# Passing on finished small operations at the end of each two-bank block of an attention kernel

## The chip, the core and the metric

The kernel runs on one NeuronCore of a Trainium2 chip. The core has a matrix engine (PE, with its weight loads shown as PEld), a vector engine (DVE), a scalar engine (ACT), a general engine (POOL) and a queue engine (SP) that issues most of the memory transfers (DMAs). The metric is the device time of one launch in microseconds (us); lower is better.

## The reference, cut to what matters

`x` has 2048 rows of 512 numbers. A modulation vector gives six rows (`sa, ca, ga, sb, cb, gb`).

```
h  = layernorm(x) * (1 + ca) + sa
x  = x + ga * (attention(h, wqkv) @ wo)      # 32 heads of 16 numbers, all 2048 rows against all 2048
h  = layernorm(x) * (1 + cb) + sb
x  = x + gb * mixer_and_mlp(h, w1, w2, w3, w4)
```

Attention is `softmax(q k^T / 4) v` for each head. What matters here is the softmax: for every query row, the kernel finds the largest score over all 2048 keys first, and subtracts it before the exponential. It does so by computing all scores twice: once to find the maxima, and once more, with the negated maximum added inside the matrix product, to feed the exponential.

## The kernel before, in words

**Units and steps.** The 2048 query rows are four chunks of 512, and the 32 heads are 16 pairs. One pair on one chunk is a *unit*: 64 units. A unit has 16 steps, one for each 128 keys; `s` counts the 1024 steps of all units. A step has two *row pairs*, one for each head: `row_pair` (L1039) puts on PE one score matmul of step `s` (`score_part`, L1037, tile `sc`) and beside it one maximum matmul of step `s + 24` (`max_part`, L1022, tile `mb`). So the maxima of a unit are computed 24 steps ahead of its scores: the last of them falls into the 8th of the 16 steps of the unit before.

**What follows on the other engines.** ACT takes the exponential of each score tile (L1033, into `pt`). A second operation on `pt` (`p_low`) runs on POOL (L1086) or, when the planner finds POOL further behind than ACT, on ACT (L158). DVE reduces each maximum tile (L1016 with two banks, 128x1024; L1014 with one). The probabilities go back to PE against `vst` (L1108, L1111), and once a unit ACT copies the accumulated result (`ac`, L1128).

**The shift rows.** When the maxima of unit `u` are complete, `max_fin` (L1053) starts a chain of small operations: DVE L1066, ACT L1068 and L1069, POOL L1070, whose result is the tile `nm`; then `shift_rows` (L1058), which issues eight small DMAs on SP (`qtl<-nm`, 1 KB each) that write the negated maxima as rows into the query tile `qtl` of unit `u`; then a mark that says so. The first score matmul of unit `u` reads those rows, so it waits for these DMAs.

**Other transfers on SP.** `load_unit(u)` (L963) issues four DMAs: two `qtl<-Qs` (96 KB each) and two `kst<-Ks` (384 KB each). There are three buffers of each, so they wait until the scores of unit `u - 3` are done. They are placed by `before` (L1606) at step `16u - 32`, which is the first step of unit `u - 2`. `load_v(u)` (L972, `vst<-Vs`, 768 KB, two buffers) is placed at step `16u - 6`. SP executes its instructions strictly in the order in which they are placed, and each waits for what it needs.

**The planner.** All this order is written out while the program is built, by a small scheduler (`Sched`). It keeps an estimated clock for each engine (`T["P"]` for PE and so on) and lists of waiting work: `chains` of small operations, `gens` (generators with background matmuls), `pend` (things to be told at a time). `misc` (L173) emits the next operations of chains that fit an engine. An entry of a chain that has no engine, such as `shift_rows` or a mark, is emitted only by `marks` (L161), and only if the planner's PE clock has passed the estimated end of the operation before it plus 200 ns:

```
    def marks(self):
        now = self.T["P"]
        ...
        for ch in list(self.chains):
            while ch[1] and ch[1][0][0] is None and ch[0] <= now:
                ch[1].pop(0)[2]()
```

Before the change `marks` has one caller, `one` (L215), which otherwise runs the next piece of a generator. `one` is called by `gap` (L205, when the planner sees a pause of 500 ns or more ahead), by `fill` (L236) and by `step` (L297), which `drain` repeats until a mark is there.

**The main loop** (from L1627 on) goes over blocks of row pairs. In the first 256 steps a block has three row pairs and one-bank maxima. From step 256 to step 994, units 16 to 61, a block has two row pairs (one step) and the maxima use two banks at once (`layout([2, 2, 1, 1, 1])`, L1693); the last 30 steps have three again. `two` is true in the middle stage. At the first row pair of a unit a block does this, in this order:

```
                if x == blk[0]:
                    before(x // 2)
                if x >= 0 and x % 32 == 0:
                    drain(("shift", x // 32))
```

and at its end, after its matmuls:

```
        elif sch.gens:
            ...
                sch.fill(due)
```

So `fill` runs only while there are generators. In the middle stage there are few: `o_fin` (L1132), eight small matmuls for a finished unit, and `tail_loads` (L1299), which is added at step 884.

Of the kernel before, what the change touches and what calls it, by code (L numbers as in the profile page):

```python
# [332 lines left out]
def kernel(ctx, tc, A_x, A_wqkv, A_wo, B_w1, B_w2, B_w3, B_w4, c, w_mod, out):  # L333
# [89 lines left out]
    sch = Sched()  # L423
# [479 lines left out]
    def drain(flag):  # L903
        while flag not in done:
            sch.step()
# [72 lines left out]
    def layout(sizes):  # L978

        while sch.owner:  # L980
            sch.step()
        bkx.close()
        psd["d"] = bkx.enter_context(tc.tile_pool(name="bk", bufs=1, space=PSUM))
        sm.sizes, sm.t = sizes, [sch.T["P"]] * len(sizes)
# [54 lines left out]
    def row_pair(s, j):  # L1039

        parts = []
        if 0 <= s < NS:
            parts.append(score_part(s, j))
        if s + LEAD < NS:
            parts.append(max_part(s + LEAD, 1 - j))

        def mms():
            for _, mm, _ in parts:
                mm()
        e = sch.put("P", CROW, max(x[0] for x in parts), mms)  # L1050
        return [partial(x[2], e) for x in parts]
# [21 lines left out]
    def p_low(s):  # L1073

        p = pt[s].rearrange("p j n -> p (j n)")
        o, i = p.bitcast(F16)[:, 0::2], p.bitcast(U16)[:, 0::2]
        ready = e_exp.pop(s) + XX
        g, a = [max(sch.T[e], ready) for e in "GA"]
        if g > a + LACT:

            for h in range(NLOW):
                n = 2 * CH // NLOW
                c = slice(h * n, (h + 1) * n)
                e_low[s] = XP["A"] + sch.crit("A", CLOW, ready, partial(act.activation, o[:, c], i[:, c], AF.Copy, scale=0.5))
        else:
            e_low[s] = XP["G"] + sch.crit("G", 1345, ready, lambda: pool.tensor_scalar(  # L1086
                o, i, 0.5, 1.0, op0=OP.mult, op1=OP.mult))

    def pv_ready(s, lo):

        return max(e_low[s], e_low[s + 1]) if lo else max(e_hi.pop(s), v_free[0] if s % NKT == 0 else 0.0)

    def pv_part(s, lo):


        u, kt = divmod(s, NKT)
        if kt == 0 and not lo:
            pv[u] = ap_.tile([P, CH], F32, name="pv", tag="v", bufs=1)
        v, acc = vst[u], pv[u]

        def mms():
            for j in range(2):
                for i in range(2):
                    r = 64 * j + 32 * i
                    if lo:
                        c = 128 + 32 * j + (0 if i else 8)
                        n = min(32, 192 - c)
                        te.matmul(acc[r:r + n, :], v[:, kt + i, c:c + n].bitcast(F16), pt[s + i].bitcast(F16)[:, j, 0::2],  # L1108
                                  start=False, stop=kt == NKT - 2, skip_group_check=True)
                    else:  # L1110
                        te.matmul(acc[r:r + 32, :], v[:, kt, r:r + 32], pt[s].bitcast(F16)[:, j, 1::2],  # L1111
                                  start=kt == 0, stop=False, skip_group_check=True)
        e = sch.put("P", CCOL, 0.0, mms)
        if lo:
            for i in range(2):
                pt.pop(s + i)
                e_low.pop(s + i)
            if kt == NKT - 2:
                acs.append((u, e + COUT))

    def ac_copy():
        u, e = acs.pop()
        while u and ("ot", u - 1) not in done:
            sch.step()
        ac = at.tile([P, CH], F32, name="ac", tag="ac", bufs=1)
        vst.pop(u)
        acc = pv.pop(u)
        e = sch.crit("A", cA(), e + PX, lambda: act.activation(ac, acc, AF.Copy))  # L1128
        v_free[0] = e + XP["A"]
        sch.add(o_fin(u, ac, e + XP["A"]), 0)  # L1130
# [168 lines left out]
    def tail_loads():  # L1299
        rings["0"] = Ring(FRONT, [], "r")  # L1300
        for _ in range(BR):
            rings["0"].add([("wr", BR)])
            yield sch.wait(T0W)
        for t in range(TPC):
            x1t[t] = fa.tile([P, D], F32, name="x1", tag="x1", bufs=X1F)
            act.dma_start(x1t[t], x_d[t * P:(t + 1) * P])
# [299 lines left out]
    def before(s):  # L1606

        nu, r = divmod(s + 32, 16)
        if r == 0 and 0 < nu < NU:
            ci, pr = units[nu]  # L1610
            drain(("kq", pr // 4))
            if ci:
                drain(("q", pr // 8))
            load_unit(nu)
        nu, r = divmod(s + 6, 16)
        if r == 0 and 0 <= nu < NU:
            drain(("v", units[nu][1] // 8))
            load_v(nu)
        if s == -12:
            unit_tiles(at, 2, dve, pool)  # L1620
# [7 lines left out]
    for k, blk in enumerate(blocks + [[]] * (LAG + CPER)):  # L1628
        if blk and blk[0] <= LENDS <= blk[-1]:
            sch.most = MOST  # L1630
        for x in blk:
            if x % 2 == 0:
# [4 lines that stand above are left out]
        if acs:  # L1637
            ac_copy()
        row = [divmod(x, 2) for x in blk if x < 2 * NS]
        s0 = row[0][0] if row else 0  # L1640
        col = []
        if k >= LAG and (k % CPER == 0 or not blk):

            x = (blocks[min(k - (LAG2 if 2 in sm.sizes else LAG), len(blocks) - 1)] or [-1])[-1]
            while pvs and 2 * (pvs[0][0] + pvs[0][1]) < x and not (col and pvs[0][0] % NKT == 0 and not pvs[0][1]):
                col.append(pvs.pop(0))
        t, start = CIN, 0.0
        two = 2 in sm.sizes
        need = 4 if two else sum((s >= 0) + (s + LEAD < NS) for s, _ in row)
        sch.flush(need)  # L1650
        banks = sorted(sm.t)
        n = 0
        for s, i in row[:2 if two else GRP]:
            n += (s >= 0) + (s + LEAD < NS)

            start = max(start, (max(sm.t[sm.take()], sm.t[sm.take(2)]) if two else banks[n - 1 + 2 * (s < 0)]) - t)
            t += CROW
        t += CROW * len(row[2:]) if two else 0.0
        t += CMID
        for s, i in col:  # L1660
            start = max(start, pv_ready(s, i) - t)
            t += CCOL
        sch.gap(start)
        sch.flush(need)
        sch.T["P"] = max(sch.T["P"], start) + CIN
        low = sorted(e_exp)
        for s, i in row:
            for fn in row_pair(s, i):
                fn()
        for x in blk[1:]:  # L1670
            if x % 2 == 0:
                before(x // 2)
        for s in low:
            p_low(s)
        sch.T["P"] += CMID
        for s, i in col:
            pv_part(s, i)
        sch.T["P"] += COUT
        for e in "ADG":
            sch.misc(e, max(sch.T["P"], sch.T[e]) + TOLE[e])  # L1680
        if s0 < 0:
            sch.fill(LEADB / 2 * len(blk))
        elif sch.gens:
            late = s0 >= NS - T0S
            due += RATE3 if late else RATE if s0 < NS // NC else RATE2
            if due >= (BURST3 if late else BURST if s0 < NS // NC else BURST2):
                sch.fill(due)
                due = 0.0
        if 2 * (NS // NC) - 1 in blk:
            for key in (("v", 1), ("kq", 3), ("q", 0), ("q", 1), "pieces"):  # L1690
                drain(key)
            qpx.close()
            layout([2, 2, 1, 1, 1])  # L1693
            sch.gapmin = GAPMIN2
            ot = o0x.enter_context(tc.tile_pool(name="ot", bufs=1, side="right"))
            for ci in range(1, NC):
                oh[ci] = ot
                osb[ci] = ot.tile([P, TPC, D], F32, name=f"osb{ci}", tag=f"osb{ci}", bufs=1)
            fa = o0x.enter_context(tc.tile_pool(name="fa", bufs=1, side="right"))
            big = {"A4": fa.tile([P, 4 * KT * 2 * P], F32R, name="A")}  # L1700
            big["A"] = big["A4"]
        if blk and blk[0] <= 2 * (NS - T0L) <= blk[-1]:
            sch.add(tail_loads())
        if blk and blk[-1] == 2 * (NS - T0S) - 1:
            layout([1] * NSM)
        if blk and blk[0] <= 2 * (NS - T0S) <= blk[-1]:
            sch.add(tail(0))
# [55 lines left out]
```

## Time and profile before

| what | us |
|---|---|
| median of 3 runs | 2565.2 (2559.43 to 2567.64) |
| the profiled execution's own time | 2569.12 |
| its span, first to last instruction | 2567.3 |
| PE busy | 2042.7 (80%) |
| DVE busy | 1637.4 (64%) |
| ACT busy | 1580.5 (62%) |
| POOL busy | 1538.0 (60%) |

The span is what the profile shows; the launch's own time is 1.8 us longer. The middle stage, from the first score matmul of unit 16 at 548.83 us to that of unit 62 at 2017.16 us, is 1468.33 us of the span. A row of a window query gives the stretch, its length, the busy time of each engine with its number of instructions in brackets, then the granted clock of PE as a share of full speed, the DMA engines' share and GB/s. In a timeline row the first number is the start, the second the length; a bracket at its end tells how long the engine had been idle before and what ended that.

### The profile page before, as it was taken

To read this page: it belongs to the slowest core of one execution; us is meant where nothing else is said; L and a number is where in the kernel's file an instruction comes from. 1 tells how busy PE (TensorE), PEld (TensorE's weight loads), DVE (VectorE), ACT (ScalarE), POOL (GpSimd) and SP (SyncE) were. 2 spreads that over 40 slices of the span, in tenths; PEclk is the share of its full clock that TensorE was granted. 3 is DMA by queue.
4 is the path that set the end of the run, shared out by engine and by line. 5 is a ranking of instruction groups with operands and counts; after the bars stand their busy time and mean duration, and the time that the engine had idled before them with its cause. 6 is when DMAs were issued, how large, how long until landed. Compare 5 with 4: busy or idle time off the path is not lost.

```text
span 2567.3 us, 40747 instructions
## 1 busy us (share of the span) xinstructions
PE 2042.7 (80%) x14456; PEld 1154.8 (45%) x14456; DVE 1637.4 (64%) x2241; ACT 1580.5 (62%) x3118; POOL 1538.0 (60%) x1455
## 2 busy tenths in 40 slices
PE   8999999976666666666666666666676889999999
PEld 5756555432222222222222222222232458888898
DVE  5688888965555555555555555555565658865543
ACT  5378877866666666666666666666676755444443
POOL 5289888975555555555555555555575755543422
PEclk9999999988787888888888888888888889999999
DMA  7777664432222222222222222222332146755352
GB/s 265 216 204 169 176 164 116 121 72 56 55 54 56 56 56 55 53 55 54 56 56 56 56 56 56 56 56 57 105 83 59 45 152 229 290 201 208 133 179 85
DMA packets 185499, 277.92 MB, mean 108 GB/s; under 512 B 117104, under 2 KB 127856, under 8 KB 169008
## 3 DMA queue, kind: packets, MB, share of 16 engines
q1 hardware_dynamic: 181792, 267.20, 38.5%
q10 hardware_dynamic: 2304, 4.20, 0.5%
q0 software_dynamic: 1200, 3.93, 0.4%
q8 instruction: 114, 1.87, 0.3%
q14 instruction: 89, 0.73, 0.1%
HBM read 211.81 MB, written 62.91 MB: 107 GB/s over the span
## 4 chain that ended last, share of the span: by engine, by line
PE 60%; DMA 19%; ACT 6%; DVE 5%; issue 4%; POOL 3%; SPq 2%; ACTq 0%; POOLq 0%; DVEq 0%
PE sc L1037 18%; DMA kst<-Ks 14%; PE pv L1111 11%; PE mb L1022 7%; PE pv L1108 4%; PE w L365 4%; PE w L361 4%; ACT pt L1033 4%; PE w L363 4%; DMA qtl<-nm 3%; SPq L137 2%; DVE mx L1014 2%; PE ot L1138 1%; POOL pt L1086 1%; POOL trs L1381 1%
## 5 line engine op out<-in xcount | busy, mean ns | idle before, releaser
L1086 POOL TENSOR_SCALAR pt<-pt 128x1024 f16<-128x1024 uint16 x920 | 1212.8, 1360 | 635.1 <-ACT pt L1033 631.8
L1033 ACT ACTIVATE pt<-sc 128x512 int32<-128x512 f32 x2048 | 1090.2, 603 | 600.7 <-PE mb L1022 576.6
L1016 DVE TENSOR_REDUCE mx<-mb 128x2 f32<-128x1024 f32 x738 | 868.7, 1219 | 576.8 <-PE mb L1022 492.5
L1037 PE MATMUL sc<-qtl,kst 64*128 64x512 f32 x2048 | 831.5, 485 | 470.2 <-DMA qtl<-nm 451.4
L1022 PE MATMUL mb<-kst,qtl 62*128 62x512 f32 x2048 | 845.1, 495 | 4.5 <-DVE vr L771 1.6
L1037 PEld LDWEIGHTS sc<-qtl,kst 64*128 64x128 f32 x2048 | 367.4, 202 | 873.4 <-issue 555.1
L1111 PE MATMUL pv<-pt,vst 128*32 128x512 f16 x4096 | 434.5, 423 | 8.1 <-ACT ac L1128 7.6
L1022 PEld LDWEIGHTS mb<-kst,qtl 62*128 62x128 f32 x2048 | 374.3, 210 | 26.1 <-DVE mx L1014 11.8
L1014 DVE TENSOR_REDUCE mx<-mb 128x1 f32<-128x512 f32 x572 | 352.0, 680 | 39.0 <-PE mb L1022 38.3
L1111 PEld LDWEIGHTS <-vst 128*32 128x32 bf16 x4096 | 104.9, 94 | 337.2 <-issue 331.1
L1108 PE MATMUL pv<-pt,vst 128*32 128x512 f16 (+1 forms) x2048 | 224.1, 420 | 1.8 <-POOL pt L1086 1.8
L1485 POOL TENSOR_TENSOR g<-sq,g 128x256 fp32r<-128x256 f32 (+1 forms) x124 | 96.5, 783 | 192.2 <-ACT g L1484 180.8
L361 PE MATMUL w<-A,wr 128*128 128x256 f32 (+1 forms) x520 | 154.5, 297 | 3.3 <-DVE sq L1463 3.3
L363 PE MATMUL w<-A,wr 128*128 128x256 f32 (+1 forms) x520 | 154.5, 297 | 0.1
L365 PE MATMUL w<-A,wr 128*128 128x256 f32 (+1 forms) x520 | 154.0, 296 | 0.0
L158 ACT ACTIVATE pt<-pt 128x1024 f16<-128x1024 uint16 x104 | 140.9, 1355 | 0.0
L1481 ACT ACTIVATE sq<-w 128x256 f32<-128x256 f32 (+1 forms) x130 | 52.0, 401 | 130.5 <-PE w L365 120.6
L365 PE MATMUL w<-wr,g 128*128 128x512 f32 x270 | 106.5, 395 | 3.1 <-POOL g L1485 3.1
L361 PE MATMUL w<-wr,g 128*128 128x512 f32 x270 | 106.9, 396 | 1.9 <-DMA wr<-Ws 1.9
L363 PE MATMUL w<-wr,g 128*128 128x512 f32 x270 | 106.2, 393 | 0.0
L361 PEld LDWEIGHTS w<-A,wr 128*128 128x128 f32 x520 | 99.8, 192 | 4.7 <-DVE sq L1463 3.5
L363 PEld LDWEIGHTS w<-A,wr 128*128 128x128 f32 x520 | 99.7, 192 | 1.5 <-DVE A L351 0.4
(157 smaller groups left out, 2185.5 us busy)
## 6 DMA issues: line engine op xcount, KB each, us to landing
wr<-Ws SPq DMA_DIRECT2D x66, 1024.0 KB, 5.3
vst<-Vs SPq DMA_DIRECT2D x64, 768.0 KB, 4.3
kst<-Ks SPq DMA_DIRECT2D x126, 384.0 KB, 6.3
Ws<-wr SPq DMA_DIRECT2D x14, 1024.0 KB, 5.2
qtl<-Qs SPq DMA_DIRECT2D x128, 96.0 KB, 4.3
Vs<-vt SPq DMA_DIRECT2D x32, 384.0 KB, 4.2
Ks<-qk SPq DMA_DIRECT2D x16, 512.0 KB, 3.7
Qs<-qk SPq DMA_DIRECT2D x16, 512.0 KB, 3.0
```

Source lines behind the costliest of these rows:

```text
L158: fn()
L361: te.matmul(o, lh, rh, start=first, stop=False)
L363: te.matmul(o, lh, rl, start=False, stop=False)
L365: te.matmul(o, ll, rh, start=False, stop=last)
L1014: end = sch.crit("D", 605, e + PX, lambda: dve.reduce_max(mxs[u][:, i, 1 - j:2 - j], b, axis=AX.X))
L1016: end = sch.crit("D", CMAX2, e + PX, lambda: dve.reduce_max(mxs[u][:, i], b, axis=AX.X))
L1022: return ready, lambda: te.matmul(b[:, k], lhs, kst[u % 3][r, c * CH:(c + 1) * CH], start=True, stop=True), after
L1033: ea = sch.crit("A", 480, e + PX, lambda: act.activation(pt[s][:, j], b[:, 0], AF.Exp))
L1037: return ready, lambda: te.matmul(b[:, 0], kst[u % 3][r, kt * P:(kt + 1) * P], qst[u][r], start=True, stop=True), after
L1086: e_low[s] = XP["G"] + sch.crit("G", 1345, ready, lambda: pool.tensor_scalar(o, i, 0.5, 1.0, op0=OP.mult, op1=OP.mult))
L1108: te.matmul(acc[r:r + n, :], v[:, kt + i, c:c + n].bitcast(F16), pt[s + i].bitcast(F16)[:, j, 0::2], start=False, stop=kt == NKT - 2, skip ...
L1111: te.matmul(acc[r:r + 32, :], v[:, kt, r:r + 32], pt[s].bitcast(F16)[:, j, 1::2], start=kt == 0, stop=False, skip_group_check=True)
```

## The change

After a block's small operations have been offered to ACT, DVE and POOL, and ahead of the fill, `marks` is called once, in blocks of the middle stage alone. It emits every finished entry without an engine: shift rows, marks of chains, and entries of `pend` that are due. Nothing else is edited.

```
--- before.py
+++ after.py
@@ -1678,6 +1678,8 @@
         sch.T["P"] += COUT
         for e in "ADG":
             sch.misc(e, max(sch.T["P"], sch.T[e]) + TOLE[e])
+        if two:
+            sch.marks()
         if s0 < 0:
             sch.fill(LEADB / 2 * len(blk))
         elif sch.gens:
```

More of the change, by code (lines that the diff above doesn't have):

```diff
@@ L1680 @@
             sch.misc(e, max(sch.T["P"], sch.T[e]) + TOLE[e])
+        if two:
+            sch.marks()
         if s0 < 0:
```

## The prediction

> **What bounds the kernel now.** I read the page first, then the waits, then the timelines of one unit boundary.
>
> ```profile
> span 2567.3 us, 40747 instructions
> ...
> PE   8999999976666666666666666666676889999999
> ...
> PEclk9999999988787888888888888888888889999999
> ...
> PE sc L1037 18%; DMA kst<-Ks 14%; PE pv L1111 11%; PE mb L1022 7%; PE pv L1108 4%; PE w L365 4%; PE w L361 4%; ACT pt L1033 4%; PE w L363 4%; DMA qtl<-nm 3%; SPq L137 2%; DVE mx L1014 2%; PE ot L1138 1%; POOL pt L1086 1%; POOL trs L1381 1%
> ```
>
> PE is full at both ends and about two thirds busy in the middle, with a lower clock there. The chain of work that ended last holds 17% of DMA, all of it in two transfers of the attention. The waits of the middle stage, and the stage's own busy times:
>
> ```profile
> PE sc L1037 <- DMA qtl<-nm: 450.8, 90, 10.4
> PEld sc L1037 <- ACT pt L1033: 222.0, 453, 1.0
> 548.83:2017.16 1468.33, 1010.74 (x7729) 413.63 (x7729) 878.46 (x828) 933.81 (x1746) 867.11 (x735) 0.82 0.28 59
> ```
>
> Columns of the last row: PE, PEld, DVE, ACT, POOL, clock. No engine is busy for more than 1011 of 1468 us. PE stands 450.8 us waiting for the shift rows, 90 times, two at a boundary: 45 boundaries, 10.0 us each. One of them, SP's queue first, then POOL, PE and the chain:
>
> ```profile
> 1202.02 0.34 SPq L137 DMA_DIRECT2D vst<-Vs  x1
> 1218.19 0.31 SPq L137 DMA_DIRECT2D qtl<-Qs  x1
> 1218.55 0.42 SPq L137 DMA_DIRECT2D kst<-Ks  x1
> 1219.39 0.30 SPq L137 DMA_DIRECT2D qtl<-Qs  x1
> 1219.74 0.41 SPq L137 DMA_DIRECT2D kst<-Ks  x1
> 1220.26 7.67 SPq L137 DMA_DIRECT2D qtl<-nm  x8
> ```
> ```profile
> 1211.21 0.20 POOL L1070 TENSOR_TENSOR nm<-mf,nm 128x8 fp32r<-128x8 f32 x1
> ```
> ```profile
> 1228.35 0.76 PE L1037 MATMUL sc<-qtl,kst 64*128 64x512 f32 x1 [9.60 <-DMA qtl<-nm]
> ```
> ```profile
> 1219.74 7.71 DMA kst<-Ks
> ```
>
> The maxima are ready at 1211.41, seven us before PE runs out of work. But the shift rows are issued at 1220.26, behind the loads for two units later, and those can only start when the unit before has finished its scores (1218.19). The shift rows then sit behind 7.7 us of `kst`. So the stall is one of order on SP, not of data. The code says why: without generators nothing calls `marks`, until the drain at the boundary, and `load_unit` is placed just ahead of that drain.
>
> **The change, part by part.**
>
> *Shift rows move ahead of the loads.* With `marks` at the end of each block they are placed when the planner's clock has passed L1070 by 200 ns, at the end of the 9th to 11th block of the unit before, not behind its 16th. The trace has this case already: unit 57, where `tail_loads` had been added and the fill called `marks` in time.
>
> ```profile
> 1851.06 0.32 SPq L137 DMA_DIRECT2D vst<-Vs  x1
> 1858.67 5.73 SPq L137 DMA_DIRECT2D qtl<-nm  x8
> 1867.19 0.32 SPq L137 DMA_DIRECT2D qtl<-Qs  x1
> 1867.56 0.42 SPq L137 DMA_DIRECT2D kst<-Ks  x1
> 1868.08 0.37 SPq L137 DMA_DIRECT2D qtl<-Qs  x1
> 1868.49 0.42 SPq L137 DMA_DIRECT2D kst<-Ks  x1
> ```
> ```profile
> 1867.02 0.40 PE L1037 MATMUL sc<-qtl,kst 64*128 64x512 f32 x1
> 1867.69 0.50 PE L1037 MATMUL sc<-qtl,kst 64*128 64x512 f32 x1
> ```
> ```profile
> DMA to landing us min/median/max: 1.9/2.0/3.4
> ```
>
> The third fence is the landing time of those eight shift rows. Issue takes SP 5.7 us, on a queue that was idle; the last is issued by 1864.4 and has landed about 2.0 later, at 1866.4, 1.3 us before unit 57 starts at 1867.69. There is no wait: 0.27 us after the last score's end (1867.42). What hides the 5.7 us of issue and the 2 us of landing is the eight blocks that PE still has; were that cover gone, they would cost 7.7 us a boundary.
>
> *Which boundaries.* The 45 are those of units 16 to 61 less 57. Unit 16's rows belong to a block of the first layout, in which `two` is false, so its wait stays: 44 are removed.
>
> *What one unit then takes.* Between stalls the clock and the pace differ:
>
> ```profile
> 1196.38:1203.41 7.03, 7.03 (x39) 2.29 (x40) 3.88 (x4) 4.25 (x9) 4.03 (x3) 0.53 0.05 8
> 1203.41:1217.67 14.26, 13.83 (x125) 5.98 (x122) 13.14 (x14) 13.29 (x27) 12.18 (x11) 1.00 0.14 52
> 1867.69:1888.65 20.96, 19.48 (x172) 8.42 (x168) 18.88 (x18) 19.87 (x39) 18.07 (x17) 1.00 0.57 130
> 1994.48:2017.16 22.68, 22.23 (x169) 9.07 (x169) 17.92 (x18) 19.64 (x37) 16.68 (x15) 0.84 0.13 36
> ```
>
> After a stall four blocks take 7.03 us at half clock (1.76 each); then eleven take 14.26 at full clock (1.30 each, ACT busy 93%). The third row is unit 57, from its first score to the end of its last, with no stall ahead of it: 20.96 us at full clock. With the 0.27 to the next unit that is 21.23, and I take **21.2 us a unit**. The last row is unit 61, which starts cold and, as the next row has no wait, ends without a stall: 22.68. I use it for unit 16.
>
> ```profile
> 2017.16 0.50 PE L1037 MATMUL sc<-qtl,kst 64*128 64x512 f32 x1
> ```
>
> Bounds: ACT is the busiest engine that does not depend on the clock, 933.81 us for 46 units, 20.3 each; below that a unit can't come without less work on ACT. Unit 57 also held a one-off that the others lack:
>
> ```profile
> 1866.64 1.40 ACTq L1306 DMA_DIRECT2D x<-in_A_x_dram  x3
> 1868.14 1.08 ACT L1033 ACTIVATE pt<-sc 128x512 int32<-128x512 f32 x2 [1.07 <-PE pv L1111]
> ```
>
> ACT issued four loads for `tail_loads` and came 1.07 us late. Without it a unit might take 20.2. Against that, backlogs on POOL and DVE that each stall lets drain now persist; the upper bound is a unit of 22.7 as the last row, its cold start replaced by other waits of that size. I stay with 21.2, between both and a whole unit as measured.
>
> *The sum.* New stage: 22.7 + 45 x 21.2 = 976.7. Old: 1468.33. Saved 491.6. The profiled execution, 2569.1, becomes 2077.5; the median of the runs is 3.9 us lower than that execution, so about **2074 us**. With 20.3 a unit: 936.2, saved 532.1, 2033. With 22.7: 1044.2, saved 424.1, 2141.
>
> *The rest of the edit.* The drain at the boundary finds its mark set and makes no step: 100 ns on the planner's clock and one offer of small operations vanish. Only the order of a few ACT, DVE and POOL operations can change by this; I cost it at nothing, since each of these operations takes 0.2 us (L1070 above) and a misplaced one is within the bounds above. Nothing else without an engine is waiting in this stage: weights are drained at L1691, before it.
>
> **What is late next.** Two queues on SP are passed. The loads for unit u+2 no longer share with shift rows, but must land before the 9th block of unit u, whose first maximum needs them. Unit 57 reached that block after 8 blocks:
>
> ```profile
> DMA to landing us min/median/max: 7.0/8.6/10.2
> ```
> ```profile
> 1878.76 0.50 PE L1037 MATMUL sc<-qtl,kst 64*128 64x512 f32 x1
> ```
>
> The first fence is the two `kst` loads issued at 1867.56 and 1868.49: the second landed at 1878.7, just as the 9th block began at 1878.76. That was with the four `x` loads in flight and a block late by 1.07. Ordinarily the second load takes 7.7 us after 1.6 us of issues, so it lands 9.3 us after the first issue; the 9th block comes at 11.07 - 1.07 = 10.0 us after the unit's start, which is itself up to 0.5 after the first issue. Spare: 0.7 to 1.2 us. The other passed load is `vst`: if the shift rows are placed ahead of it, it moves from the unit's 4th block to behind their issue. It would land some 2 us after the boundary, with its first use in the 4th block, 3.4 us or more after it, and so would share the first 2 us with `kst`.
>
> Does a `vst` load hold up `kst`? In the first stage it was issued behind it by 3 us:
>
> ```profile
> kst<-Ks SPq DMA_DIRECT2D x2, 384.0 KB, 6.0
> vst<-Vs SPq DMA_DIRECT2D x1, 768.0 KB, 6.9
> ```
>
> `kst` kept its 6 us (median), `vst` took the delay. The Trainium skill, DMA: Bandwidth & Descriptors, section "Queues, rings and completion order", says that each DMA engine takes one queue's descriptors in the order they were put in, and takes turns between queues. By that rule a later `vst` on SP's queue can't delay `kst`, while the `x` loads of ACT's queue can; these rows agree.
>
> **The rivals.**
>
> *B, a new transfer wait.* The `kst` load, or the last shift rows, land late in most units. For it: the spare of about 1 us, and `vst` ahead of `kst` if the order comes out so. Against it: the row above, and unit 57 waited for neither. Price 1 to 4 us a unit, say 2: 45 x 2 = 90, **2164 us**.
>
> *C, the clock stays low.* PE has no long pause any more, but many short ones (453 waits for ACT of up to 1.0 us). If it ran at the 1.76 us blocks throughout, a unit takes 16 x 1.76 = 28.2, the stage 1292, saved 177: **2388 us**. Against it: the eleven blocks and unit 57 have such pauses at clock 1.00. The Trainium skill, TensorE: Matmul & The Clock Gate, section "A second HAM failure mode: psum-queue depth-cycling", tells of a matmul stream cycling through PSUM banks whose micro-pauses make the clock fall back again and again, which by itself would bring this case. The trace does not bear it out.
>
> *D, it doesn't do what it says.* The chain isn't ripe by the planner's clocks before the boundary, so the rows stay behind the loads: **2565 us**. Against it: in units 57 and 62 one call in about seven blocks was enough.
>
> *E, slower.* As C, at PE's clock, with the weight loads and the maxima at half clock exposed as they are at a cold unit's start, of which this row holds four, with the first and its waits, 2.05 us each:
>
> ```profile
> 1195.19:1203.41 8.22, 7.82 (x41) 2.61 (x42) 3.88 (x4) 4.57 (x9) 4.03 (x3) 0.52 0.05 7
> ```
>
> That is 16 x 2.05 = 32.8 a unit, 46 of them 1509, 41 more than now: **2606 us**. It decides from 1468.33 / 736 = 1.99 us a block on. Unit 57's 20.96 / 16 = 1.31 speaks against it.
>
> **How the numbers follow.** Forecast (a unit of 20.2 to 22.7, no new wait) 0.75; B 0.17; C 0.02; D 0.03; E 0.02; something else 0.01. The forecast's own range is 2030 to 2141. B begins there; I take its nearer half in, and give 2028 to 2155. What can be told from no change is about 0.3%, 8 us. Faster: forecast, B, C and part of the rest, 0.95; within 0.3%: D, 0.03; slower: E, 0.02.
>
> **What would show it.** Shift rows issued about 8 us before each boundary, ahead of `qtl<-Qs`; the wait of L1037 for `qtl<-nm` down from 450.8 to some 10 us (unit 16); a clock near 1.00 in the stage; units of about 21 us, ACT over 90% busy, PE's waits being for ACT. A wait of L1022 for `kst` would show B. A unit of more than 22.7 us, or a stall left at the boundaries, makes the prediction wrong.

## The result and the profile after

The changed kernel takes 2058.0 us (2055.0 to 2060.6, four runs) against 2566.4 us of the kernel before on the same chip: a ratio of 0.802, 95% interval 0.799 to 0.8045. The prediction was 2074 us, in a range of 2028 to 2155. The page of the changed kernel, the lines that answer to those of before:

```profile
span 2057.8 us, 40834 instructions
...
PE   8999999999799999999999999999998899999999
...
PEclk9989999999899999999999999999999999999999
...
PE sc L1037 17%; PE pv L1111 12%; ACT pt L1033 9%; PE mb L1022 8%; PE w L365 5%; PE w L361 5%; PE w L363 5%; PE pv L1108 4%; POOL pt L1086 3%; DVE mx L1014 2%; ACT pt L158 2%; PE ot L1138 2%; ACT ac L1128 1%; DMA wr<-Ws 1%; POOL trs L1381 1%
```

The hollow in the middle of PE's row is gone, the clock is full, and no transfer of the attention is left in the chain. The middle stage by the window view: the whole of it, then unit 16, then units 30 and 31.

```profile
546.98:1503.29 956.31, 908.32 (x7730) 391.95 (x7730) 872.93 (x828) 913.38 (x1746) 862.27 (x735) 1.00 0.43 90
546.98:569.82 22.84, 21.91 (x170) 9.16 (x170) 18.14 (x18) 18.41 (x36) 17.36 (x15) 0.87 0.14 36
838.87:859.90 21.03, 19.94 (x172) 8.59 (x168) 19.02 (x19) 19.99 (x39) 19.35 (x17) 1.00 0.41 86
859.90:880.29 20.39, 19.50 (x172) 8.41 (x168) 18.97 (x19) 19.77 (x39) 18.30 (x17) 1.00 0.45 89
```

The stage fell from 1468.33 to 956.31 us, by 512 us; the rest of the span grew by 2.5. Units alternate between 21.0 and 20.4 us. The engines do nearly the same work as before (DVE 873 of 878 us, POOL 862 of 867, ACT 913 of 934), in two thirds of the time; PE's busy time fell by 102 us, because its matmuls no longer run at half clock after each stall.

SP's timeline at two boundaries, and the waits of the stage:

```profile
843.42 0.34 SPq L137 DMA_DIRECT2D vst<-Vs  x1
852.37 4.98 SPq L137 DMA_DIRECT2D qtl<-nm  x8
859.41 0.31 SPq L137 DMA_DIRECT2D qtl<-Qs  x1
859.77 0.42 SPq L137 DMA_DIRECT2D kst<-Ks  x1
860.29 0.37 SPq L137 DMA_DIRECT2D qtl<-Qs  x1
860.70 0.55 SPq L137 DMA_DIRECT2D kst<-Ks  x1
864.43 0.34 SPq L137 DMA_DIRECT2D vst<-Vs  x1
872.15 5.89 SPq L137 DMA_DIRECT2D qtl<-nm  x8
```
```profile
PEld sc L1037 <- ACT pt L1033: 203.0, 414, 1.0
PE sc L1037 <- ACT pt L1033: 36.0, 68, 0.7
PE pv L1111 <- ACT ac L1128: 11.5, 45, 1.4
PE sc L1037 <- DMA qtl<-nm: 10.4, 2, 10.0
```

The shift rows now stand between `vst` and the next loads, and the 450.8 us of PE's wait for them are 10.4, at one boundary: unit 16's. The lists of instructions of the two kernels show the change in its purest form: on PE, DVE, ACT and POOL the order is the same, instruction for instruction (on PE, neighbours that start within 0.02 us of each other may change places); on SP alone it differs. All 512 us come from the place of eight small DMAs in one queue.

### The profile page after: what moved, and what is told of

It is laid out like the page before. It is cut to its first block, busy times and chain, and to the rows that moved or that the text cites. A ratio compares the mean times of both kernels' runs of the same rounds, so it can differ in the third digit from the quotient of the medians.

```text
span 2057.8 us, 40834 instructions
## 1 busy us (share of the span) xinstructions
PE 1944.5 (94%) x14456; PEld 1136.9 (55%) x14456; DVE 1632.3 (79%) x2241; ACT 1560.6 (76%) x3118; POOL 1533.5 (75%) x1455
## 4 chain that ended last, share of the span: by engine, by line
PE 65%; ACT 14%; DVE 6%; issue 6%; POOL 5%; DMA 3%; SPq 1%; ACTq 0%; POOLq 0%; DVEq 0%
PE sc L1037 17%; PE pv L1111 12%; ACT pt L1033 9%; PE mb L1022 8%; PE w L365 5%; PE w L361 5%; PE w L363 5%; PE pv L1108 4%; POOL pt L1086 3%; DVE mx L1014 2%; ACT pt L158 2%; PE ot L1138 2%; ACT ac L1128 1%; DMA wr<-Ws 1%; POOL trs L1381 1%
## 5 line engine op out<-in xcount | busy, mean ns | idle before, releaser
L1037 PE MATMUL sc<-qtl,kst 64*128 64x512 f32 x2048 | 763.3, 450 | 54.1 <-ACT pt L1033 37.6
L1022 PE MATMUL mb<-kst,qtl 62*128 62x512 f32 x2048 | 777.4, 460 | 4.5 <-DVE vr L771 1.6
L1037 PEld LDWEIGHTS sc<-qtl,kst 64*128 64x128 f32 x2048 | 341.4, 185 | 410.0 <-ACT pt L1033 229.3
L1111 PE MATMUL pv<-pt,vst 128*32 128x512 f16 x4096 | 410.6, 400 | 14.0 <-ACT ac L1128 13.9
L1022 PEld LDWEIGHTS mb<-kst,qtl 62*128 62x128 f32 x2048 | 349.8, 193 | 26.1 <-DVE mx L1014 11.8
L1108 PE MATMUL pv<-pt,vst 128*32 128x512 f16 (+1 forms) x2048 | 210.8, 389 | 1.8 <-POOL pt L1086 1.8
L361 PEld LDWEIGHTS w<-A,wr 128*128 128x128 f32 x520 | 100.8, 194 | 5.0 <-DVE sq L1463 3.5
L1463 DVE SCALAR_TENSOR_TENSOR sq<-sq,w 128x256 f32<-128x256 f32 (+1 forms) x130 | 58.2, 449 | 56.3 <-ACT sq L1483 56.1
```

Of the source, the lines that this page charges most:

```text
L361: te.matmul(o, lh, rh, start=first, stop=False)
L1022: return ready, lambda: te.matmul(b[:, k], lhs, kst[u % 3][r, c * CH:(c + 1) * CH], start=True, stop=True), after
L1037: return ready, lambda: te.matmul(b[:, 0], kst[u % 3][r, kt * P:(kt + 1) * P], qst[u][r], start=True, stop=True), after
```

## The experiments

The kernels of this table are explained below it, one by one. Means over units 18 to 55, worked out from the traces: the gap is from the end of a unit's last score matmul to the first of the next, the run from a unit's first score matmul to the end of its last.

| kernel | gap, us | run, us | middle stage, us | total, us |
|---|---|---|---|---|
| before | 10.02 | 22.38 | 1468.3 | 2566 |
| changed | 0.27 | 20.46 | 956.3 | 2058.0 |
| swap | 0.27 | 20.46 | 955.1 | 2045.0 |
| u16 | 0.27 | 20.47 | 956.1 | 2045.6 |
| warm | 10.05 | 22.06 | 1476.2 | 2576.4 |
| warm42 | 10.21 | 20.76 | 1427.7 | 2529.8 |
| actq | 8.60 | 22.09 | 1409.0 | 2516.7 |
| lead22 | 0.27 | 21.40 | 1000.3 | 2116.6 |
| lead28 | 0.27 | 24.88 | 1159.0 | 2273.2 |
| x_act | 0.27 | 23.65 | 1097.9 | 2200.2 |
| x_pe | 0.27 | 22.30 | 1040.6 | 2140.1 |
| x_pool | 0.27 | 20.98 | 978.8 | 2077.9 |
| lact500 | 0.27 | 20.96 | 975.7 | 2061.6 |

The totals of swap, u16, lact500 and the changed kernel are medians of four executions, the others are single ones; the kernel before had medians of 2566 to 2574 beside them.

**The place on SP alone.** On the kernel before:

```
-                if x == blk[0]:
-                    before(x // 2)
                 if x >= 0 and x % 32 == 0:
                     drain(("shift", x // 32))
+                if x == blk[0]:
+                    before(x // 2)
```

> The kernel before with two statements exchanged: at a unit's first row pair the drain for the shift rows comes ahead of the placing of the loads (before). The rows are still passed on only at the boundary, never by a call at the end of a block. Theory (all that counts is where the rows stand on SP relative to the four loads of unit u+2): the waits of units 17 to 61 go as in the changed kernel, and unit 16's too, which is 10 us of wait and about 1.6 us of cold start more: 2058 - 11.6 = about 2046 us. Rival (the rows must be passed on some blocks ahead of the boundary): issue and landing, 5.7 + 2.0 = 7.7 us, stay exposed at 45 boundaries, so 2058 + 347 = about 2400 us.

2045.0 us, ratio 0.7965 (0.795 to 0.798). The rows are passed on only at the boundary, and still SP issues them as early as in the changed kernel (at 529.39, 8.3 us before the boundary at 537.65; 7.5 and 8.1 us in the rows above), since an instruction on SP waits for its data, not for its neighbours on other engines. SP's timeline, then the stage:

```profile
520.36 0.34 SPq L137 DMA_DIRECT2D vst<-Vs  x1
529.39 5.31 SPq L137 DMA_DIRECT2D qtl<-nm  x8
536.08 0.32 SPq L137 DMA_DIRECT2D qtl<-Qs  x1
...
541.53 0.34 SPq L137 DMA_DIRECT2D vst<-Vs  x1
550.27 4.98 SPq L137 DMA_DIRECT2D qtl<-nm  x8
557.75 0.31 SPq L137 DMA_DIRECT2D qtl<-Qs  x1
```
```profile
537.65:1492.70 955.05, 906.43 (x7729) 391.55 (x7730) 873.27 (x828) 914.08 (x1747) 863.40 (x736) 1.00 0.43 91
```

The rows at 529.39 are those of unit 16's boundary, which the change doesn't reach and the exchange does. The theory holds, the rival falls: what counts is not when the planner passes the rows on, but ahead of what.

**The changed kernel once more, and unit 16.**

> The changed kernel as it is, on the same chip as the others: 2058 us, within 0.3%. Its middle stage again 956 us.

2055.8 us, ratio 0.8006 (0.7992 to 0.8019); stage 956.0.

```
-        if two:
+        if two or s0 >= 240:
             sch.marks()
```

> The changed kernel with the call also in blocks from step 240 on (two or s0 >= 240), which are the last blocks of the first layout and hold unit 16's shift rows. Theory: the one stall that is left, at unit 16 (10 us of wait, about 1.6 us of cold start), goes: about 2046 us. Rival (unit 16 is held by the drains and the new PSUM layout at step 256 in any case): 2058 us, the wait then put down to something else.

2045.6 us, ratio 0.7964 (0.7949 to 0.7979): 10 us below the changed kernel on the same chip, as expected. Swap and u16 are the best of the study, and can't be told apart.

**The cold clock by itself.** On the kernel before, at the second row pair of a unit's last block in the middle stage, the maximum matmul is repeated; it writes the same values again.

```
         def mms():
             for _, mm, _ in parts:
                 mm()
+            if s % NKT == NKT - 1 and j == 1 and 16 * NKT <= s < NS - T0S and s + LEAD < NS:
+                for _ in range(NWARM):
+                    parts[1][1]()
```

With 36 repeats:

> The kernel before, with the last maximum matmul of each unit of the middle stage repeated 36 times (it writes the same values into the same bank), so that PE works for some 8 of the 10 us of each stall. The stall itself stays. This measures the cold clock by itself. Theory: the change saved 512 us in the stage, of which 44 x 10.0 = 441 are the waits and the other 71, 1.6 us a stall, the four blocks at half clock after it; so with a warm clock 45 x 1.6 = 73 us are saved: about 2493 us, first blocks of a unit at clock 1.00. Rival (the slow first blocks come from engines that start empty, not from the clock): no change, 2565 us, or some us more if the repeats outlast the stall.

2576.4 us, no gain: by the total, the rival's result. But the clock still fell. The first four blocks of units 36 and 39 in that run:

```profile
1187.80:1195.68 7.88, 7.27 (x40) 2.49 (x41) 3.87 (x4) 4.36 (x8) 3.85 (x3) 0.57 0.05 4
1283.05:1289.46 6.41, 5.08 (x41) 1.95 (x41) 4.71 (x5) 5.23 (x10) 3.04 (x3) 1.00 0.07 12
```

Ahead of unit 36, PE stood still for 1.4 us between the end of the repeats and the landing of the rows, ahead of unit 39 for 0.4. The run doesn't tell the two theories apart, so the pause was closed with 42 repeats:

> As warm, with 42 repeats. In warm the 36 repeats took 8.55 us and left pauses of about 1.2 us, and the clock still fell to half for one or two steps of 3.41 us at most unit starts. 42 repeats take 10.0 us and leave next to none. Theory (the cold clock is the part of the saving beyond the wait): every unit starts at clock 1.00, and its run, from the first score matmul to the end of the last, falls from 22.4 us to about 20.7 us; the total by 45 x 1.7 = 76 us less what the repeats outlast the stall, up to 0.5 us a unit: 2490 to 2520 us. Rival (the first blocks are slow because the engines behind PE start empty): runs stay at 22 us, total 2565 us or above.

The run of a unit fell from 22.38 to 20.76 us, at a stall as long as before (10.21). Unit 36 in the kernel before (whose row to 1218.41 has 23.22 us at clock 0.83) and in this one:

```profile
1195.19:1218.41 23.22, 22.39 (x168) 8.96 (x168) 17.76 (x17) 18.44 (x36) 16.95 (x15) 0.83 0.10 35
```
```profile
1167.02:1187.79 20.77, 19.40 (x167) 8.63 (x166) 18.69 (x18) 18.19 (x36) 16.83 (x15) 1.00 0.13 39
```

The total is 43.8 us below the kernel before (2573.6 on that chip), less than expected. Summed over the trace, the runs of units 16 to 61 lost 71 us; but the repeats lengthen the gap at the 44 stalls by 11 us in all, and at the two boundaries that have no stall, those of units 57 and 62, they cost 10 us each: 71 - 11 - 20 = 40 in the stage (1468.3 to 1427.7). The part by itself is the run: 1.6 us a stall. With it the 512 us are 427 of gap (44 stalls) and 85 of run, of which 71 are shown to be the clock. The other 14 are most likely the clock too: 8 units of warm42 still hold a step at half clock and run for 22.2 us in the mean, the 38 others for 20.6, near the changed kernel's 20.5.

**Another queue in place of another order.** On the kernel before:

```
-                        sch.dma(dma.dma_start,
+                        sch.dma((act if u > 16 else dma).dma_start,
```

> The kernel before with the shift rows of units 17 to 63 issued by ACT in place of SP, at the same late place in the program: they no longer stand behind the loads on SP, but behind ACT's last exponentials, and they share the DMA engines with kst. Theory (the order in one queue makes the 10 us): the rows start about 1 us after the last score, take 8 x 0.45 us of issue and 2 us to land, more while kst is in flight: a stall of 6 to 8 us, total 2430 to 2500 us. Rival (it is the traffic of kst, whatever the queue): a stall of 9 us or more, 2540 us or above.

2516.7 us: between the two. The gap fell only from 10.0 to 8.6 us, nearer to the rival's 9 than to the theory's 6 to 8.

```profile
PE sc L1037 <- DMA qtl<-nm: 390.2, 73, 9.7
```

One boundary of each kernel, issue and landing in us, read from the trace:

```
            before, all on SP            actq, rows on ACT
            issued    landed             issued    landed
kst 1       1218.55   1223.28            1183.30   1188.74
kst 2       1219.74   1227.45            1185.28   1191.20
row 1       1220.26   1227.65            1183.21   1188.20
row 2       1220.78   1227.84            1183.74   1189.08
row 3       1221.48   1228.02            1184.39   1191.16
row 4       1222.07   1228.21            1185.05   1191.38
row 7       1224.18   1228.78            1189.27   1192.02
row 8       1227.47   1229.35            1190.39   1192.46
```

A row that lands 2.0 us after its issue when no load is in flight (the median of the changed kernel) took 5.0 to 6.8 us on ACT's queue, if issued before the first `kst` load had landed (rows 1 to 5), and rows 2 to 4 landed with or just behind a `kst` load, though they are not behind it in any queue. The unit's first score matmul needs rows 1 to 4; it ran at 1191.63, 0.25 us after row 4 had landed. The order on SP is thus only how the rows came to be late; what makes them late is that the loads are already in flight. The theory as I had put it, one queue's order, doesn't hold; "issued after the loads" stands in its place.

**How near the next transfer waits are.** On the changed kernel, `LEAD = 22`, then `LEAD = 28` in place of 24; this shifts the maxima in the first stage too, so the middle stage is what to read.

> The changed kernel with the maxima 22 steps ahead in place of 24: the shift rows are ready two blocks, 2.3 us, later before each boundary, and the kst load has two blocks more. In the changed kernel the last shift row lands 1.2 us before the unit starts (0.4 to 1.9). Theory: the rows then land about 1 us late, and since the second score matmul alone needs the last four of them, 0.5 to 1 us of wait for qtl<-nm a unit: 2080 to 2105 us. Rival (the rows have more spare than that, since the first unit's rows are all the first score needs): 2058 us.

2116.6 us, above the expected range. The stage alone, 1000.3 us, 44 more, would lie in it, but not by the expected way:

```profile
PE sc L1037 <- ACT pt L1033: 59.8, 88, 1.7
...
PE sc L1037 <- DMA qtl<-nm: 5.8, 5, 1.7
```
```profile
868.41 1.36 ACT L158 ACTIVATE pt<-pt 128x1024 f16<-128x1024 uint16 x1
869.62 2.06 ACT L1033 ACTIVATE pt<-sc 128x512 int32<-128x512 f32 x4
```
```profile
869.10 0.50 PE L1037 MATMUL sc<-qtl,kst 64*128 64x512 f32 x1
...
870.26 0.50 PE L1037 MATMUL sc<-qtl,kst 64*128 64x512 f32 x1 [0.66 <-ACT pt L1033]
```

The rows hardly cost anything (5.8 us in all): the rival, that they have more spare than 1.2 us, is right. PE waits for ACT, whose `p_low` now falls on the boundary. That is about half of the 44 us; the rest goes with the clock. By the trace, 13 of the 46 units hold a step of 3.41 us at half clock and run for 22.6 us in the mean, the 33 others for 21.0, where the changed kernel has 20.5. Units 30 and 31, which do the same work:

```profile
869.10:891.68 22.58, 21.02 (x172) 8.60 (x169) 19.36 (x19) 20.05 (x39) 18.91 (x17) 0.92 0.39 80
891.68:912.87 21.19, 19.63 (x172) 8.45 (x168) 19.17 (x19) 19.92 (x39) 18.81 (x17) 1.00 0.39 86
```

The 15 us beyond the stage are in the first stage.

> The changed kernel with the maxima 28 steps ahead: the first maximum of unit u+2 comes four blocks, 4.5 us, earlier in unit u, while its kst load can't start earlier. In the changed kernel that load lands 2.6 us ahead of its first use (1.2 at least). Theory (rival B of the prediction lay just outside: two to three blocks away): a wait for kst of some 2 us in each unit, 45 x 2 = 90 us: about 2150 us, with L1022 or the weight load waiting for kst. Rival (a unit's wait there is made up for elsewhere, since ACT sets the pace): less than 30 us.

2273.2 us; stage 1159.0 us, 203 more, twice what I expected.

```profile
PE mb L1022 <- DMA kst<-Ks: 114.6, 46, 4.1
```
```profile
916.72:921.52 4.80, 4.56 (x44) 1.91 (x41) 4.80 (x5) 4.70 (x11) 4.80 (x4) 1.00 0.94 178
921.52:928.20 6.68, 4.42 (x26) 1.57 (x22) 2.72 (x4) 3.04 (x8) 2.98 (x4) 0.64 0.16 22
```

The wait is there, 2.5 us in each unit, near to the 2 us expected. The rest follows it: the second row, two blocks with the wait in front, runs at clock 0.64. A pause of 2.5 us costs nearly as much again in the blocks behind it (203 us are 4.4 a unit).

**What sets the pace now.** Each of the next three adds small work to one engine, unknown to the planner, for units 17 to 61 (x_pe for all of the stage):

```
+            for _ in range(8 if 16 < u < 62 else 0):
+                act.activation(scr, mf, AF.Copy)          # x_act, behind L1069
+            if s % NKT == 11 and j == 1 and 16 * NKT <= s < NS - T0S:
+                for _ in range(8):
+                    parts[1][1]()                         # x_pe
+            for _ in range(8 if 16 < u < 62 else 0):
+                pool.tensor_tensor(scr, mf, mf, op=OP.add)  # x_pool, behind L1070
```

> The changed kernel with eight more small ACT operations a unit (copies of the 128x8 tile mf to a scratch tile, right behind L1069), units 17 to 61; the planner does not know of them and all orders stay. In the changed kernel's stage ACT is busy 95.5%, PE 95.0%, DVE 91.3%, POOL 90.2%. Theory (ACT sets the pace of 20.7 us a unit): 8 x 0.2 = 1.6 us a unit more, 45 x 1.6 = 72 us: about 2128 us. Rival (PE sets it, and ACT's 5% idle takes them): under 25 us more.

> The changed kernel with one maximum matmul repeated eight times a unit in its 12th block (same values into the same bank), 8 x 0.24 = 1.9 us of PE a unit. Theory (ACT sets the pace; PE's 5% of waits for ACT take part of it): about 1 us a unit at most, 0 to 45 us more. Rival (PE sets it): 1.9 us a unit, 45 x 1.9 = 86 us more, 2144 us.

> The changed kernel with eight more small POOL operations a unit (128x8 additions into a scratch tile, behind L1070), 8 x 0.2 = 1.6 us of POOL a unit, the time that POOL has to spare (20.7 x 9.8% = 2.0 us). Theory (ACT sets the pace): under 0.4 us a unit, 0 to 18 us more: 2058 to 2076 us. Rival (POOL's lag, through the pt buffers, is what holds ACT and PE): 1.6 us a unit, 2130 us.

Stages, in that order:

```profile
546.60:1644.49 1097.89, 982.43 (x7728) 408.02 (x7728) 879.72 (x828) 988.15 (x2106) 866.86 (x735) 0.91 0.38 79
```
```profile
547.58:1588.16 1040.58, 990.71 (x8097) 454.91 (x8098) 874.14 (x828) 916.60 (x1746) 867.29 (x735) 1.00 0.40 83
```
```profile
547.32:1526.15 978.83, 936.41 (x7729) 399.23 (x7730) 879.16 (x828) 913.95 (x1746) 926.08 (x1095) 1.00 0.42 88
```

POOL's 64 us cost 22.5 in the stage: mostly hidden, though the total is 2 us above the expected range. ACT's 75 us cost 142, more than either expectation; PE's 82 us cost 84, the rival's price. So neither "ACT sets the pace" nor "PE sets it" is right: both do, in turns. I read it so: in a block without extra work on ACT the matmuls follow each other without a pause, and what is added to PE there is paid in full; where ACT has its `p_low`, its copy of `ac` or the added copies, PE stands, and that is paid in full too. No run put the added matmuls into a block with such work on ACT, so this is not shown. ACT's double price is the clock again: in every other unit of x_act PE stands 2.1 us in one piece, in the others 0.9, and 34 units hold a step at half clock and run for 24.25 us in the mean. The units with added copies and without such a step run for 21.9, 1.4 more than in the changed kernel. Unit 30, then 31:

```profile
897.97 0.79 PE L1037 MATMUL sc<-qtl,kst 64*128 64x512 f32 x1 [2.12 <-ACT pt L1033]
```
```profile
882.22:907.32 25.10, 22.09 (x173) 9.10 (x170) 19.16 (x19) 21.66 (x47) 19.11 (x17) 0.86 0.35 72
907.32:929.51 22.19, 20.06 (x173) 8.49 (x170) 19.00 (x19) 21.33 (x47) 18.23 (x16) 1.00 0.40 82
```

The last takes ACT work away instead, on the swap kernel: `LACT = 500.0` in place of 200.

> The exchanged-statements kernel (swap, 2045 us) with the planner's threshold LACT for giving p_low to ACT at 500 in place of 200: 85 of them on ACT in place of 104 in all, so 0.3 to 0.4 fewer a unit on ACT and as many more on POOL. Theory (ACT sets the pace): 0.35 x 1.25 = 0.4 us a unit less, 2045 - 20 = 2025 us. Rival (POOL and ACT are balanced as they stand): no change or slower, 2045 to 2065 us.

2061.6 us, ratio 0.8021 (0.8008 to 0.8034): 16 us slower than swap, which ran on another chip (ratio 0.7965).

```profile
538.52:1514.21 975.69, 912.06 (x7728) 395.42 (x7728) 876.89 (x828) 901.90 (x1732) 882.04 (x751) 0.99 0.43 89
```

ACT lost 12 us of work (901.90 against swap's 914.08), and the stage gained 21. This is in line with the three before: the sum of one engine's work does not tell the pace of a stage in which two engines hold each other by turns. Which blocks the fewer `p_low` now hit, and why that is worse, I did not trace further; it stays open.

## Why the prediction was right

*What bounds the kernel, and why.* Right. PE's wait for the shift rows was the stall, it came from the order on SP, and the order is all that changed. The prediction put the delay down to the rows sitting behind 7.7 us of `kst`. That was incomplete: actq shows that they are late on another queue too, as long as the loads are in flight. The clock's part of each stall, 1.9 us of the unit behind it, was in the forecast through the warm unit that it took as its measure; warm42 shows that most of it is the clock.

*Where the rows go.* Right: SP issues them about 8 us before each boundary (852.37 for 859.90, 872.15 for 880.29), and no wait is left. The last row of unit 57 had landed by 1865.81, not 1866.4: the 2.0 us of a landing count from the start of its issue. They stayed behind `vst`; the case in which `vst` has to wait behind them did not come.

*Which boundaries.* Right: 44 waits are gone, unit 16's is there (10.4 us), and swap and u16 show what it is worth, 10 to 11 us of the total.

*What one unit takes.* This is the term that was mis-sized: 21.2 us forecast, (956.31 - 22.84) / 45 = 20.74 measured. 45 x 0.46 = 21 us too much, which is the difference between the forecast stage (976.7) and the measured one (956.3). The 1.07 us that ACT lost in unit 57 to issuing four loads was in the sample and is not in other units; the prediction named it and kept it in. The changed kernel's own unit 57, which still has these loads, ran for 20.98 us, as the sample did (20.96), and the units around it for 20.5 in the mean. ACT's busy time, which the text took for a lower bound of 20.3 a unit, fell itself to 19.9: the same operations took 913 us in place of 934. Unit 16, 22.7 forecast, took 22.84.

*The sum.* 491.6 us forecast, 512 in the stage.

*What is late next.* The prediction gave `kst` a spare of 0.7 to 1.2 us. It was larger, 2.4 us in the median by the trace, from the landing of the second load to the 9th block: that load lands in 7.0 us (median of the stage), not 7.7, without rows issued right behind it, and is issued sooner after the first.

lead28 shows that B was not far away all the same: four blocks earlier, 4.5 us, the wait is 2.5 us a unit. The rule weighed there, that a later `vst` can't delay `kst` on the same queue, was not tested by itself.

*The rivals.* D fell with the first trace. C and E fell too, for this kernel: its stage has 414 short waits of weight loads for the exponential, 68 of matmuls for it and 45 for the copy of `ac`, of 1.4 us at most, and the clock stays at 1.00. But their mechanism is close by: pauses of 0.8 to 4.1 us in one piece, in warm, x_act and lead28, do lower it, and in lead22 it fell in some units that had no pause of more than 0.7 us.

*What the signs were.* Clock 1.00, ACT busy 95.5% (913.38 of 956.31), PE's waits for ACT: as forecast. That ACT sets the pace, which the text took for its lower bound of a unit, is part of the truth: time added to PE is paid in full as well.

## What to carry to other kernels

When an engine waits for a small transfer, look at the issue queue first: compare when its data were ready with when it was issued, and see what stands ahead of it and what that waits for. An in-order queue needs the small urgent transfer ahead of the large one that waits for later work; how early the program places it mattered little beyond that here (swap), and another queue hardly helped once the large one was in flight (actq). Price a removed stall by a unit of the same trace that happens to have none, take its one-offs out, and count the half-clock blocks behind each stall.

## What the runs showed of the hardware that was not expected

**A DMA on another queue lands with the loads in flight.** The rows on ACT's queue took 5.2 us in the median to land, at the boundary of the table, against 2.0 us in the changed kernel, where they are issued ahead of the loads.

```profile
DMA to landing us min/median/max: 2.1/5.2/6.8
```

The Trainium skill, DMA: Bandwidth & Descriptors, section "Queues, rings and completion order", says that the mark of a finished DMA is written only after every earlier write of that DMA engine, across its queues. The landings of actq agree: rows 2 and 3, issued 0.65 us apart, landed 2.1 us apart, each within 0.4 us of a `kst` load's landing.

**Issue can wait for an older transfer's end.** In the kernel before, the eighth row was issued at 1227.47, 3.3 us after the seventh and 0.02 us after the second `kst` had landed. In the trace both have the same completion semaphore, so the issue waited for its earlier use. The same shows at other places: 86 of the 512 rows of the kernel before were issued within 0.06 us after the landing of a `kst` load with their semaphore, 2 in the changed kernel. That is inferred from the traces; no run varied it.

**Short pauses can lower the clock.** Pauses of PE of 0.8 to 2.0 us in warm, 0.9 and 2.1 in x_act and 2.1 to 4.1 in lead28 were followed by stretches at half clock of 3.41 us or twice that, as the trace records them: after nearly all of them in warm and lead28, after all of the 2.1 us and about half of the 0.9 us ones in x_act. The length of a pause alone doesn't decide. In lead22 ten of the 13 half-clock steps had no pause of more than 0.7 us in the 6.8 us before them, and most such pauses there were followed by none; in the changed kernel no pause in the stage behind unit 16 was, one of 1.4 us included (unit 17). What decides is open.
